# First block on whole float32 weights, weight splits moved to the second block, activation in two ScalarE steps, written-out order for the first block

## The chip, the cores and the metric

One core of a Trainium2 chip runs the whole program. The metric is device microseconds of one execution. TensorE multiplies, VectorE, ScalarE and GpSimd do elementwise work, and SyncE issues the DMAs. The kernel before took 884.1, 885.01 and 887.9 us in three runs, median 885.01.

## The reference

Attention without a softmax over the scores: `q` goes through a softmax over the head's 64 channels, `k` through one over the 576 positions, and out = q_s (k_sᵀ v). The result, 2304 tokens by 512, goes through two layers of the same shape:

```python
h = x @ w_in                       # 2304x512 @ 512x2048
g = where(h >= 1, h, where(h <= -1, 0, (h + 1)**2 / 4))
x = g @ w_out                      # 2304x2048 @ 2048x512
h = x @ w_in2
x = (h * tanh(log1p(exp(h)))) @ w_out2
```

The four weight matrices arrive as float64 and all else as float32. The kernel rebuilds each weight as float32 from its two 32-bit words.

## The kernel before, in words

The tokens are cut into six blocks of 384, the 2048 hidden channels into 16 chunks `c` of 128. The first layer runs in slots, one for each block `n` and chunk: `gemm1` (x times w_in, four slices of 128 channels into a bank `h`), the activation `act1`, `split_g`, and three slots later `gemm2` (w_out times g into four banks `acc`). While a block is worked on, the attention of later tokens is filled in between (tasks `kv_task` and `q_task`, one stage at a time). The second layer follows the sixth block; the change does not touch it.

A float32 product is made in one of two ways. `three` (L419) takes operands that were split into a high and a low part of the type float32r and issues three products. A plain float32 product is one line of code and two instructions in the trace. The kernel before uses the plain form in `gemm2` of the first block for the chunks under `WHOLE` = 8, and splits everywhere else.

A weight passes these stages (`w_stages`, 128x512 values at a time): DMA into `wraw`; VectorE `words` (L128, L132) builds a float32 magnitude from the two words; ScalarE rounds (L137), takes the sign (L138) and the magnitude (L143); `signed` multiplies the two (L155), on VectorE for most chunks and on GpSimd for the early ones; `w_parts` copies the high part on ScalarE (L202) and subtracts it on GpSimd (L204). A class `Line` moves the weights on by a stage per tick. In the first block all 32 weights of layer one pass through it; those of layer two follow, one every second slot.

The activation is three ScalarE steps from `h` (L459 to L461: half of the magnitude, half minus that and not under zero, square) and one on VectorE (L462). From chunk 8 on g is split too (L451, L452).

The order of the startup is a string, `STARTUP`, in which `p` with a number stands for that many products with the identity that fill TensorE's time. `REGIONS` says on which engines the order of issue is the order in the program: none up to slot 16, SyncE and ScalarE up to slot 80, all after that. Where it is not, a scheduler orders the instructions.

Of the kernel before, what the change touches and what calls it, by code (L numbers as in the profile page):

```python
# [18 lines left out]
P = 128  # L19
# [5 lines left out]
LEAD = 7  # L25
WHOLE = 8
REGIONS = [([], 0), ([], 16), (["sync", "scalar"], 16 * 5), (None, 16 * 6 + LAG)]
# [13 lines left out]
def tile_attention_two_moes(  # L41
# [77 lines left out]
    def w_stages(ph, c, m):  # L119
# [5 lines left out]
        def words():  # L125
# [10 lines left out]
            sg = f(t)[:, :, 1]  # L136
            nc.scalar.activation(out=sg, in_=sg, func=AF.Copy, bias=ROUND)  # L137
            nc.scalar.activation(out=sg, in_=sg, func=AF.Sign, bias=unround)  # L138

        def signed():  # L140
            t = f(st.pop("t"))
            w, sg = t[:, :, 0], t[:, :, 1]
            nc.scalar.activation(out=w, in_=w, func=AF.Abs)  # L143
            to = w
            if ph == 2:
                if c < NF // 2:
                    quarters[m, c] = big([P, 2, 2, 2 * P], F32, "wq")
                to = quarters[m, c % (NF // 2)][:, c * 2 // NF].rearrange("p c x -> p (c x)")
            elif m == 1 and c < WHOLE:
                if c % 2 == 0:  # L150
                    whole[c // 2] = big([P, 2, DM], F32, "whole")
                to = whole[c // 2][:, c % 2, :]
            st["w"] = to
# [3 lines left out]
        def split():  # L157
            if m == 0 or c >= WHOLE:
                w_parts(ph, c, m, st["w"])
# [33 lines left out]
        if ph == 1:  # L193
            return [words, signed, split]
        return [words, signed, sums, last_sum, store] if u >= 0 else [words, signed]
# [4 lines left out]
    def w_parts(ph, c, m, w, dve=False):  # L200
        t = parts[ph, c, m] = big([P, 2, DM], F32R, "parts")
        nc.scalar.activation(out=t[:, 0, :], in_=w, func=AF.Copy)  # L202
        eng = nc.vector if dve else nc.gpsimd
        eng.tensor_tensor(out=t[:, 1, :], in0=w, in1=f(t[:, 0, :]), op=ALU.subtract)  # L204
# [4 lines left out]
    def x_tiles(ph, n):  # L209
        xh[ph, n] = [small([P, 2, TB], F32R, "xh") for _ in range(NP // 2)]  # L210
# [10 lines left out]
    def by_rows(a, b, c, j0, nj, name):  # L221
# [17 lines left out]
    def kv_task(b, c):  # L239
# [4 lines left out]
        def load():  # L244
            st["k"], st["e"] = zip(*(by_rows(k, b, c + i, 0, J, "k_t") for i in two))
# [42 lines left out]

        def exps():
            st["e"] = [exp_tile(e, J, "k_e") for e in st["e"]]  # L290
            for i in two:
                kt = st["k"][i]
                mb = st["mb"][:R, i * P:(i + 1) * P].rearrange("p (h d) -> p h d", h=2)
                nc.vector.tensor_tensor(
                    out=kt, in0=kt, in1=mb.unsqueeze(2).to_broadcast([R, 2, J, D]), op=ALU.subtract
                )
                nc.scalar.activation(
                    out=st["e"][i].rearrange("p j h d -> p h j d"), in_=kt, func=AF.Exp
                )
# [26 lines left out]
        if not ready:  # L326
            return [load, load_v, rows_max, m_transpose, col_max, m_rows, exps, product, scaled]
# [5 lines left out]
    def q_task(b, c, nc_, j0, nj, n, o):  # L333
# [4 lines left out]
        def load():  # L338
            t = rows_tile("q_t")[:, :2 * nc_ * nj]
            if ready:  # L340
# [14 lines left out]
        def exps():  # L355
            g = st["g"]
            mx = sp.tile([R, 2 * J], F32, tag="qm", name="qm")[:, :2 * nc_ * nj]
            nc.vector.tensor_reduce(out=mx, in_=g, axis=AX.X, op=ALU.max)
            nc.gpsimd.tensor_tensor(
                out=g, in0=g, in1=mx.unsqueeze(2).to_broadcast([R, 2 * nc_ * nj, D]), op=ALU.subtract  # L360
            )
            if "e" in st:
# [9 lines left out]
        def scaled():  # L372
            g = st["e"].rearrange("p c j h d -> p (c j h) d")
            s = sp.tile([R, 2 * J], F32, tag="qs", name="qs")[:, :2 * nc_ * nj]
            nc.vector.tensor_reduce(out=s, in_=g, axis=AX.X, op=ALU.add)
            nc.vector.tensor_scalar_add(s, s, EPS)
            nc.vector.reciprocal(out=s, in_=s)
            nc.gpsimd.tensor_tensor(
                out=g, in0=g, in1=s.unsqueeze(2).to_broadcast([R, 2 * nc_ * nj, D]), op=ALU.mult
            )  # L380

# [21 lines left out]
        def x_split():  # L403
            ps = st["x"][:, :nc_ * w].rearrange("p (c t) -> p c t", c=nc_)
            if (1, n) not in xh:
                x_tiles(1, n)
            cs = slice(c % 2, c % 2 + nc_)
            hi, lo = xh[1, n][c // 2][:, cs, o:o + w], xl[1, n][c // 2][:, cs, o:o + w]
            nc.scalar.activation(out=hi, in_=ps, func=AF.Copy)
            nc.vector.tensor_tensor(out=lo, in0=ps, in1=f(hi), op=ALU.subtract)  # L410

        if not ready:
            return [load, exps, scaled, None, transposed, copied, product, x_split]
# [18 lines left out]
    def gemm1(s):  # L432
        ph, n, c = s
        hs[s] = h_p.tile([P, 512], F32, tag="h", name="h")
        for kc in range(NP):
            ks = slice(kc * P, (kc + 1) * P)
            three(
                hs[s][:, :TB], parts[ph, c, 0][:, 0, ks], parts[ph, c, 0][:, 1, ks],
# [571 lines left out]
```

## Time and profile before

| | |
|---|---|
| median of three runs | 885.01 us |
| the profiled execution | 884.33 us |
| its span | 882.5 us |
| TensorE busy | 847.6 us (96%) |
| VectorE, ScalarE, GpSimd busy | 570.2, 543.5, 412.6 us |

The span runs from the first to the last instruction that the profile shows; 1.83 us lie outside it. "Busy" of TensorE counts overlapping products until the modelled end of each, so a group's length is read from the start of one group to the start of the next.

### The profile page before, as it was taken

Reading aid. Unit: us, or ns where it says so; the run is one execution under the profiler, and the core shown is the slowest. Engines: PE = TensorE matmul, PEld = TensorE weight load, DVE = VectorE, ACT = ScalarE, POOL = GpSimd, SP = SyncE. Lnnn points to the kernel's source line nnn. Section 1 sums busy time; section 2 is a strip of 40 time slices with the busy share of each in tenths; the row PEclk is TensorE's granted clock in tenths of the full one; section 3 lists DMA queues with packets and bytes.
Section 4 is the critical chain, followed back from the end, with each engine's and each line's share of the span. In section 5 each row is a group of like instructions: output and inputs, shape, how many; then the busy total and the mean of one; then the engine's idle time right before and its main releaser. Section 6 shows DMA issues by size and latency. Waiting matters only on the chain. (4 is left out here: it accounts for less than half of the span.)

```text
span 882.5 us, 15027 instructions
## 1 busy us (share of the span) xinstructions
PE 847.6 (96%) x5308; PEld 820.9 (93%) x5308; DVE 570.2 (65%) x916; ACT 543.5 (62%) x953; POOL 412.6 (47%) x376
## 2 busy tenths in 40 slices
PE   7879779999999999999998999999999999999998
PEld 7756679899999999999998999999999999999998
DVE  6998975854756577475324636765667669656453
ACT  1899889877777777786756844442444466553521
POOL 2663666865645455364355316558555468000000
PEclk9799999999999999999999999999999999999999
DMA  9986221544664362354359238777876888866933
GB/s 251 325 235 166 72 58 51 170 134 131 163 186 135 105 206 94 117 170 141 110 206 341 61 102 272 253 269 286 306 247 248 317 316 293 279 225 197 305 113 103
DMA packets 139996, 171.27 MB, mean 194 GB/s; under 512 B 57360, under 2 KB 109584, under 8 KB 139920
## 3 DMA queue, kind: packets, MB, share of 16 engines
q1 hardware_dynamic: 139680, 170.10, 60.0%
q8 instruction: 42, 0.69, 0.3%
q14 instruction: 34, 0.28, 0.1%
q10 hardware_dynamic: 240, 0.20, 0.1%
HBM read 108.40 MB, written 61.87 MB: 193 GB/s over the span
## 5 line engine op out<-in xcount | busy, mean ns | idle before, releaser
L489 PE MATMUL acc<-ghl,parts 128*128 128x384 f32 x1056 | 204.0, 341 | 5.3 <-POOL v_t L250 2.6
L489 PEld LDWEIGHTS acc<-ghl,parts 128*128 128x128 f32 x1056 | 184.7, 189 | 7.6 <-POOL v_t L250 2.9
L690 PE MATMUL o<-w2p,gc 128*128 128x256 f32 x1296 | 152.8, 280 | 0.4 <-ACT gc L531 0.3
L690 PEld LDWEIGHTS o<-w2p,gc 128*128 128x128 f32 x1296 | 152.1, 189 | 0.8 <-ACT gc L531 0.8
L452 POOL TENSOR_TENSOR ghl<-rg,ghl 128x384 fp32r<-128x384 f32 x87 | 97.7, 1124 | 113.6 <-ACT ghl L451 110.5
L420 PE MATMUL h<-xh,parts 128*128 128x384 f32 x384 | 136.0, 354 | 7.6 <-DVE rg L462 7.6
L462 DVE SCALAR_TENSOR_TENSOR rg<-h,rg 128x384 f32<-128x384 f32 x96 | 53.2, 554 | 138.7 <-ACT rg L461 136.3
L422 PE MATMUL h<-xh,parts 128*128 128x384 f32 x384 | 132.2, 344 | 2.7 <-POOL parts L204 2.7
L421 PE MATMUL h<-xl,parts 128*128 128x384 f32 x384 | 131.5, 343 | 0.0
L531 ACT ACTIVATE gc<-gq 128x768 fp32r<-128x768 f32 x84 | 69.9, 843 | 64.0 <-DMA gq<-gd 43.5
L534 DVE TENSOR_TENSOR gc<-gq,gc 128x768 fp32r<-128x768 f32 x84 | 89.9, 1109 | 27.9 <-ACT gc L531 20.8
L421 PE MATMUL m<-xc,w2p 128*128 128x384 f32 x288 | 97.1, 337 | 1.3 <-DVE xc L534 1.3
L420 PE MATMUL m<-xc,w2p 128*128 128x384 f32 x288 | 97.1, 337 | 0.2 <-ACT xc L531 0.2
L422 PE MATMUL m<-xc,w2p 128*128 128x384 f32 x288 | 96.8, 336 | 0.0
L459 ACT ACTIVATE rg<-h 128x384 f32<-128x384 f32 x96 | 46.8, 487 | 63.1 <-PE h L422 61.1
L420 PEld LDWEIGHTS h<-xh,parts 128*128 128x128 f32 x384 | 73.7, 192 | 12.6 <-DVE rg L462 10.0
L627 ACT ACTIVATE high<-high 128x768 f32<-128x768 f32 x24 | 20.3, 847 | 94.2 <-DVE high L198 42.5
L422 PEld LDWEIGHTS h<-xh,parts 128*128 128x128 f32 x384 | 73.6, 192 | 4.7 <-POOL parts L204 4.5
L421 PEld LDWEIGHTS h<-xl,parts 128*128 128x128 f32 x384 | 73.7, 192 | 1.3
L132 DVE SCALAR_TENSOR_TENSOR wraw<-wraw 128x512 uint32<-128x512 uint32 x64 | 70.3, 1099 | 1.3
L198 POOL TENSOR_TENSOR s<-high 128x384 f32<-128x384 f32 x24 | 26.5, 1106 | 81.0 <-ACT high L627 81.0
L460 ACT ACTIVATE rg<-rg,half 128x384 f32<-128x384 f32 x96 | 59.4, 618 | 2.6
(110 smaller groups left out, 1562.3 us busy)
## 6 DMA issues: line engine op xcount, KB each, us to landing
gq<-gd SPq DMA_DIRECT2D x84, 384.0 KB, 6.1
gd<-s SPq DMA_DIRECT2D x48, 384.0 KB, 3.3
wraw<-in_moe_w_in_dram SPq DMA_DIRECT2D x32, 512.0 KB, 4.8
wraw<-in_moe_w_out_dram SPq DMA_DIRECT2D x32, 512.0 KB, 4.0
gd<-low SPq DMA_DIRECT2D x24, 384.0 KB, 3.8
wk<-ws SPq DMA_DIRECT2D x32, 256.0 KB, 2.1
w<-wk SPq DMA_DIRECT2D x16, 384.0 KB, 4.4
v_t<-in_v_dram SPq DMA_DIRECT2D x32, 144.0 KB, 3.4
```

The source lines that it names most:

```text
L132: nc.vector.scalar_tensor_tensor(out=t[:, :, 0], in0=t[:, :, 1], scalar=3, in1=t[:, :, 0], op0=ALU.logical_shift_left, op1=ALU.bitwise_xor,)
L420: nc.tensor.matmul(ps, ah, bh, start=start, stop=False)
L421: nc.tensor.matmul(ps, ah, bl, start=False, stop=False)
L422: nc.tensor.matmul(ps, al, bh, start=False, stop=stop)
L452: eltwise(s).tensor_tensor(out=gl[s], in0=g, in1=f(gh[s]), op=ALU.subtract)
L459: nc.scalar.activation(out=r, in_=h, func=AF.Abs, scale=0.5)
L460: nc.scalar.activation(out=r, in_=r, func=AF.Relu, scale=-1.0, bias=half)
L462: nc.vector.scalar_tensor_tensor(out=g, in0=h, scalar=0.0, in1=r, op0=ALU.max, op1=ALU.add)
L489: nc.tensor.matmul(acc[key][x][:, :TB], *pairs[at], start=first and at == 0, stop=last and at == 2)
L531: nc.scalar.activation(out=hi, in_=x, func=AF.Copy)
L534: eng.tensor_tensor(out=lo, in0=x, in1=f(hi), op=ALU.subtract)
L690: nc.tensor.matmul(ps[j][:, :QUARTER], a[:, c, js], b, start=i == c == which == 0 and b is wh, stop=i == pairs[-1] and c == which == 1,)
```

## The change

1. Layer one, first block (n = 0): x is not split, and `gemm1` and `gemm2` use the plain float32 form for all 16 chunks, on weights kept in `whole` tiles. The weights are not split in this block.
2. The weights of layer one are split in the second block: in slot c `w_high` copies and `w_low` subtracts for the w_in chunk c + 3 (subtraction on VectorE) and the w_out chunk c (on GpSimd). The first three w_in chunks are split at the end of the first block.
3. The activation is two ScalarE steps (a Relu with scale and bias, a square) and one on VectorE that takes max with 1 and min with the square. This holds in all blocks.
4. All multiplications of magnitude and sign of layer one are on GpSimd.
5. The weights of layer two start in the middle of the second block, two in three slots.
6. `STARTUP` now holds everything up to the end of the first block, with the attention of the second batch (names in capitals), and every engine keeps that order.

```diff
-REGIONS = [([], 0), ([], 16), (["sync", "scalar"], 16 * 5), (None, 16 * 6 + LAG)]
+AHEAD = 3
+REGIONS = [(["sync", "scalar"], 16 * 5), (None, 16 * 6 + LAG)]
 STARTUP = (
...
+    "w8.words w4.abs act0.c w4.mul w12.L w3.rnd act0.g w6.rnd w7.words w13.L Q0.L Q1.L G0 w3.sgn w6.sgn w10.words "
...
-            eng = nc.vector if (m if ph == 2 else c > (1 if m else 8)) else nc.gpsimd
-            eng.tensor_tensor(out=to, in0=w, in1=sg, op=ALU.mult)
+            eng = nc.vector if ph == 2 and m else nc.gpsimd
+            eng.tensor_tensor(out=to, in0=t[:, :, 0], in1=t[:, :, 1], op=ALU.mult)
...
+    def w_high(c, m):
...
+        t = parts[c, m] = big([P, 2, DM], F32R, "parts")
+        nc.scalar.activation(out=t[:, 0, :], in_=whole[m, c // 2][:, c % 2, :], func=AF.Copy)
+
+    def w_low(c, m):
+        t, w = parts[c, m], whole[m, c // 2][:, c % 2, :]
+        eng = nc.gpsimd if m else nc.vector
+        eng.tensor_tensor(out=t[:, 1, :], in0=w, in1=f(t[:, 0, :]), op=ALU.subtract)
...
+            if n == 0:
+                nc.tensor.matmul(
+                    hs[s][:, :TB], whole[0, c // 2][:, c % 2, ks], xh[ph, n][kc // 2][:, kc % 2, :],
+                    start=kc == 0, stop=kc == NP - 1,
+                )
+                continue
...
     def as_whole(s):
-        return s[:2] == (1, 0) and s[2] < WHOLE
+        return s[:2] == (1, 0)
...
-        nc.scalar.activation(out=r, in_=h, func=AF.Abs, scale=0.5)
-        nc.scalar.activation(out=r, in_=r, func=AF.Relu, scale=-1.0, bias=half)
-        nc.scalar.activation(out=r, in_=r, func=AF.Square)
-        nc.vector.scalar_tensor_tensor(out=g, in0=h, scalar=0.0, in1=r, op0=ALU.max, op1=ALU.add)
...
+        nc.scalar.activation(out=t[:, 0, :], in_=hs[s][:, :TB], func=AF.Relu, scale=0.5, bias=half)
...
+        nc.scalar.activation(out=r, in_=r, func=AF.Square)
...
+        nc.vector.scalar_tensor_tensor(
+            out=g, in0=hs[s][:, :TB], scalar=1.0, in1=r, op0=ALU.max, op1=ALU.min
+        )
...
-            elif ph == 1 and (n < NB - 1 or line.items):
-                w_tick(2 if c % 2 else 1)
...
+            if (n > 1 or n == 1 and c >= NF // 2) and (n < NB - 1 or line.items):
+                w_tick(i % 3)
...
+            if n == 1:
+                w = [(x, m) for x, m in ((c + AHEAD, 0), (c, 1)) if x < NF]
```

On TensorE the startup before runs as follows (`warm` is a product with the identity, `mT` and `mb` belong to the maxima of k, `kv` to the product of k and v, `qT` are transposes of q, `xps` is x before it is copied out):

```order
L841 MATMUL warm<-ident 128x128 x20
L268 MATMUL mT<-ident,km 128x96 x4
L841 MATMUL warm<-ident 128x128 x3
L284 MATMUL mb<-ident,mx 96x128 x2
L841 MATMUL warm<-ident 128x128
L284 MATMUL mb<-ident,mx 96x128 x2
L841 MATMUL warm<-ident 128x128 x34
L305 MATMUL kv<-v_t,k_e 128x130 x12
L386 MATMUL qT<-ident,q_e 128x96 x8
L305 MATMUL kv<-v_t,k_e 128x130 x12
L386 MATMUL qT<-ident,q_e 128x96 x8
L401 MATMUL xps<-qt,kvs_85 128x384 x2
```

and the changed kernel's startup runs so:

```order
L944 MATMUL warm<-ident 128x128 x33
L309 MATMUL mT<-ident,km 128x96 x2
L944 MATMUL warm<-ident 128x128 x12
L309 MATMUL mT<-ident,km 128x96 x2
L325 MATMUL mb<-ident,mx 96x128 x4
L944 MATMUL warm<-ident 128x128 x34
L351 MATMUL kv<-v_t,k_e 128x130 x24
L452 MATMUL qT<-ident,q_e 128x96 x8
L467 MATMUL xps<-qt,kvs_85 128x384
L452 MATMUL qT<-ident,q_e 128x96 x4
L467 MATMUL xps<-qt,kvs_86 128x384
L467 MATMUL xps<-qt,kvs_85 128x384
```

More identity products stand ahead of the first maxima, the two products of k and v stand together, and none of the transposes lies between them.

In the first block, TensorE's rows of the kernel before, around the first `gemm2` (L420 to L422 are `three`, L478 the plain form):

```order
L420 MATMUL h<-xh,parts 128x384
L421 MATMUL h<-xl,parts 128x384
L422 MATMUL h<-xh,parts 128x384
L478 MATMUL acc<-rg,whole 128x384 x4
L420 MATMUL h<-xh,parts 128x384
L421 MATMUL h<-xl,parts 128x384
L422 MATMUL h<-xh,parts 128x384
```

and the changed kernel's (L514 is `gemm1` on whole weights, L571 `gemm2`):

```order
L514 MATMUL h<-x_412,whole 128x384 x2
L514 MATMUL h<-x_413,whole 128x384 x2
L571 MATMUL acc<-rg,whole 128x384 x4
L514 MATMUL h<-x_412,whole 128x384 x2
L514 MATMUL h<-x_413,whole 128x384 x2
L571 MATMUL acc<-rg,whole 128x384 x4
L514 MATMUL h<-x_412,whole 128x384 x2
L514 MATMUL h<-x_413,whole 128x384 x2
L571 MATMUL acc<-rg,whole 128x384 x4
```

A slot of before has 12 products of split operands and four whole ones (12 split ones from chunk 8 on); a slot of the change has eight whole ones.

On ScalarE, a slot of the first block before (L202 is the copy of a weight's high part, L459 to L461 the activation):

```order
L137 ACTIVATE wraw<-wraw 128x512
L459 ACTIVATE rg<-h 128x384
L138 ACTIVATE wraw<-wraw,unround 128x512
L460 ACTIVATE rg<-rg,half 128x384
L143 ACTIVATE wraw<-wraw 128x512
L461 ACTIVATE rg<-rg 128x384
L202 ACTIVATE parts<-wraw 128x512
L137 ACTIVATE wraw<-wraw 128x512
L143 ACTIVATE wraw<-wraw 128x512
L138 ACTIVATE wraw<-wraw,unround 128x512
```

and the changed kernel's (L162, L166, L170 are round, sign and magnitude, L539 and L543 the activation):

```order
L162 ACTIVATE wraw<-wraw 128x512 x2
L166 ACTIVATE wraw<-wraw,unround 128x512 x2
L170 ACTIVATE wraw<-wraw 128x512
L539 ACTIVATE rg<-h,half 128x384
L170 ACTIVATE wraw<-wraw 128x512
L543 ACTIVATE rg<-rg 128x384
L162 ACTIVATE wraw<-wraw 128x512 x2
L166 ACTIVATE wraw<-wraw,unround 128x512 x2
```

The copy and one step of the activation have gone from the slot, and two weights pass in each.

## Rows read from the trace of the kernel before

**Rows 1.** Stages: busy of each engine (instructions), granted clock, DMA share, GB/s

```profile
core 0: us, PE busy (x) PEld busy (x) DVE busy (x) ACT busy (x) POOL busy (x), PEclk, DMA share, GB/s
22.00:34.00 12.00, 11.77 (x63) 11.50 (x64) 11.96 (x23) 9.16 (x16) 9.04 (x8) 0.57 0.98 312
38.00:158.00 120.00, 101.17 (x508) 86.77 (x507) 100.99 (x152) 111.41 (x209) 71.86 (x59) 0.96 0.47 132
158.00:600.00 442.00, 437.63 (x2530) 428.80 (x2529) 262.00 (x442) 295.19 (x545) 228.61 (x216) 1.00 0.53 170
```

**Rows 2.** TensorE's waits from 38 to 158 us: total, times, longest

```profile
PE h L420 <- DVE rg L462: 7.1, 4, 3.8
PE qT L386 <- DVE kvs L321: 3.4, 1, 3.4
...
PE acc L489 <- POOL v_t L250: 2.6, 1, 2.6
```

**Rows 3.** TensorE's timeline, first block and start of the second: start, duration

```profile
37.87 0.63 PE L421 MATMUL h<-xl,parts 128*128 128x384 f32 x1
...
55.66 2.74 PE L478 MATMUL acc<-rg,whole 128*128 128x384 f32 x8
58.20 0.41 PE L420 MATMUL h<-xh,parts 128*128 128x384 f32 x1
58.45 0.34 PE L421 MATMUL h<-xl,parts 128*128 128x384 f32 x1
...
152.66 0.34 PE L420 MATMUL h<-xh,parts 128*128 128x384 f32 x1
...
154.76 0.51 PE L489 MATMUL acc<-ghl,parts 128*128 128x384 f32 x2
...
157.61 0.34 PE L420 MATMUL h<-xh,parts 128*128 128x384 f32 x1
```

**Rows 4.** TensorE's timeline, startup

```profile
1.58 7.13 PE L841 MATMUL warm<-ident 128*128 128x128 f32 x40 [1.58 <-POOL ident masks.py:199]
...
12.76 7.76 PE L841 MATMUL warm<-ident 128*128 128x128 f32 x68
22.22 4.15 PE L305 MATMUL kv<-v_t,k_e 96*128 96x130 f32 x24 [1.71 <-issue]
```

**Rows 5.** TensorE's timeline, key-value products of the second batch

```profile
111.49 2.84 PE L305 MATMUL kv<-v_t,k_t 96*128 96x130 f32 x24
114.09 1.98 PE L489 MATMUL acc<-ghl,parts 128*128 128x384 f32 x10
```

**Rows 6.** ScalarE's groups by form, first 160 us: busy, mean

```profile
L460 ACT ACTIVATE rg<-rg,half 128x384 f32<-128x384 f32 x20 | 12.5, 623 | 0.2
```

**Rows 7.** ScalarE's timeline, one weight in the first block

```profile
46.18 0.70 ACT L143 ACTIVATE wraw<-wraw 128x512 f32<-128x512 f32 x1
46.74 0.78 ACT L138 ACTIVATE wraw<-wraw,unround 128x512 f32<-128x512 f32 x1
47.39 0.69 ACT L137 ACTIVATE wraw<-wraw 128x512 f32<-128x512 f32 x1
```

**Rows 8.** Instructions on raw weights, first 60 us: min/median/max ns

```profile
L128 DVE TENSOR_SCALAR wraw<-wraw x14: 413/430/4524, 18.0 to 59.1; 128x512 uint32<-128x512 uint32 x14
...
L132 DVE SCALAR_TENSOR_TENSOR wraw<-wraw x13: 678/694/2417, 18.4 to 56.3; 128x512 uint32<-128x512 uint32 x13
...
L155 POOL TENSOR_TENSOR wraw<-wraw x5: 1036/1221/1485, 28.5 to 54.3; 128x512 f32<-128x512 f32 x5
...
L204 POOL TENSOR_TENSOR parts<-wraw,parts x5: 1296/1304/1504, 31.3 to 57.3; 128x512 fp32r<-128x512 f32 x5
```

**Rows 9.** VectorE's groups by form, first 160 us: busy, mean

```profile
L132 DVE SCALAR_TENSOR_TENSOR wraw<-wraw 128x512 uint32<-128x512 uint32 x34 | 39.1, 1151 | 0.6
L128 DVE TENSOR_SCALAR wraw<-wraw 128x512 uint32<-128x512 uint32 x34 | 24.1, 712 | 3.7 <-DMA wraw<-in_moe_w_in_dram 2.1 <-DMA wraw<-in_moe_w_out_dram 1.6
...
L462 DVE SCALAR_TENSOR_TENSOR rg<-h,rg 128x384 f32<-128x384 f32 x19 | 10.5, 550 | 9.4 <-ACT rg L461 9.3
```

More of the change, by code (lines that the diff above doesn't have):

```diff
@@ L193, in w_stages, with first, second @@
         if ph == 1:
-            return [words, signed, split]
-        return [words, signed, sums, last_sum, store] if u >= 0 else [words, signed]
+            return dict(words=words, rnd=rounded, sgn=sign, abs=magnitude, mul=signed)
+        def first():
+            words()
+            rounded()
+            sign()
+        def second():
+            magnitude()
+            signed()
+        return [first, second, sums, last_sum, store] if u >= 0 else [first, second]
     def add(eng, out, a, b, sub=True):
         eng.tensor_tensor(out=out, in0=a, in1=b, op=ALU.subtract if sub else ALU.add)
[L200 to L203, printed above, removed]
+    def w_high(c, m):
[4 more added lines that the diff above has]
+        eng = nc.gpsimd if m else nc.vector
         eng.tensor_tensor(out=t[:, 1, :], in0=w, in1=f(t[:, 0, :]), op=ALU.subtract)
@@ L324, in scaled @@
                 )
-        if not ready:
-            return [load, load_v, rows_max, m_transpose, col_max, m_rows, exps, product, scaled]
+        if b < 2:
+            return dict(
+                L=load, V=load_v, max=rows_max, mT=m_transpose, mx=col_max, mb=m_rows, s0=partial(below, 0),
+                s1=partial(below, 1), e0=partial(exp, 0), e1=partial(exp, 1), kv=product, sc=scaled,
+            )
         return [
@@ L478, in gemm2 @@
                 nc.tensor.matmul(
-                    a[:, :TB], whole[c // 2][:, c % 2, x * P:(x + 1) * P], gh[s], start=first, stop=last
+                    a[:, :TB], whole[1, c // 2][:, c % 2, x * P:(x + 1) * P], gh[s], start=first, stop=last
                 )
@@ L801, in drain @@
                 self.step()
-    ahead = [(1, c, m) for c in range(NF) for m in range(2)]
-    ahead += [(2, c, m) for m in range(2) for u in range(NF // 2) for c in (u, u + NF // 2)]
+    ahead = [(2, c, m) for m in range(2) for u in range(NF // 2) for c in (u, u + NF // 2)]
     todo = list(ahead)
@@ L807, in tile_attention_two_moes, with w_ahead, w_tick @@
     fill = None
-    def w_ahead(upto):
-        while ahead and ahead[0][0] <= upto and len(raws) < (4 if upto == 1 else 1):
+    def w_ahead():
+        while ahead and len(raws) < 1:
             w_load(*ahead.pop(0))
-    def w_tick(upto):
-        line.tick(w_stages(*todo.pop(0)) if todo and todo[0][0] <= upto else None)
+    def w_tick(new):
+        line.tick(w_stages(*todo.pop(0)) if todo and new else None)
     def region(engines):
@@ L955, in tile_attention_two_moes @@
         put(places, end - 6 + 2 * i if i < 3 else end - 1, g_split, 0, i)
-    with region(REGIONS[0][0]):
+    with region(None):
         startup()
-    at = 0
-    for engines, upto in REGIONS[1:]:
+    at = NF
+    for engines, upto in REGIONS:
         with region(engines):
```

181 lines of the change are left out of this document (108 added, 73 removed), and 28 rows, old and new, of the table STARTUP.

## The prediction

> **What bounds the kernel now.** I read the busy time by stages first, then TensorE's waits, then its timeline where the change begins and ends, then the groups on ScalarE and VectorE there. From 158 to 600 us TensorE is busy 437.6 of 442 us: it sets the time, and a faster ScalarE or VectorE can win 4.4 us there at the very most [rows 1]. From 38 to 158 us it is busy 101 of 120, and even this counts overlapped ends; ScalarE is busy for 111 of the 120 us and VectorE for 101 [rows 1]. So the weights' conversion and splitting hold TensorE back there. Its longest waits are for VectorE's last step of the activation (7.1 us in four waits), for the scaled k-v products (3.4) and for a tile of v (2.6) [rows 2]. The rest is lost in the startup: between 22 and 34 us the granted clock is 0.57, mostly the lower of the levels 1.2 and 2.4 GHz, after TensorE had idled 1.7 us ahead of the first k-v product, whose 24 instructions then took 4.15 us [rows 1, 4]. The same 24 take 2.6 us at the full clock, from 111.49 to 114.09 [rows 5].
>
> The sum is made between two points that both kernels have: the start of the first `gemm1`, and the start of `gemm1` for the fifth chunk of the second block, which stands at 157.61 us [rows 3]. Behind that point TensorE has the same products to do in both kernels.
>
> **What a product costs.** A split `gemm1` or `gemm2` is 12 instructions and takes 2.10 us (152.66 to 154.76) [rows 3]. A whole one is eight instructions: they start at 55.66, and the second split product behind them starts at 58.45; less the 0.17 us of the one product between, they take 2.62 us [rows 3]. So a whole chunk costs 0.52 us more than a split one.
>
> Before, the stretch from 37.87 to 157.61 us holds 20 `gemm1` (16 of the first block, four of the second) and eight split `gemm2` of the first block with one of the second, 29 × 2.10 = 60.9 us; eight whole `gemm2`, 21.0 us; and the products of the second batch's attention. Of these the k-v products are two groups of 24, 2 × 2.6 = 5.2 us [rows 5]; the transposes, maxima and projections I estimate at as much again, so 10 us together. The sum is 92 of 119.7 us: some 28 us are waits and half clock.
>
> After, the same stretch holds 32 whole groups, 32 × 2.62 = 83.8 us, five split ones, 10.5, and the same 10: 104.3 us. The change thus adds 12.6 us of products (24 × 0.52), in exchange for waits.
>
> **What happens to ScalarE.** One weight takes it 0.56 + 0.65 + 0.56 us from start to start (magnitude, sign, and rounding like the magnitude) = 1.77 us [rows 7]. Two weights pass in a slot: 3.54 us. The Relu with a bias lasts 0.62 us and overlaps its neighbour by some 0.12, so 0.5, and the square no more [rows 6, 7]. That is 4.5 us in a slot whose products take 5.24. Before, the copy of the high part and the third step came on top, 0.6 to 0.9 and 0.4 us, against products of 4.7. ScalarE passes from bound to covered. VectorE has two weights at 0.43 + 0.69 us undisturbed [rows 8], at 0.71 + 1.15 as they were on average [rows 9], and 0.55 for the activation [rows 9]: 2.8 to 4.3 us. GpSimd has two multiplications of 1.04 to 1.49 us each [rows 8]. Both are under 5.24 with the attention's work on top, but VectorE not by much. If that cover goes, a slot grows by what is missing; the second rival prices it.
>
> **Startup.** The first group of 40 warm-up products ran from 1.58 to about 8.5 us, the later one of 68 in 7.8 us, 0.114 each [rows 4]. Now 66 come first, which puts the first maxima at 8.5 + 26 × 0.1 = 11 us; 24 more, the second maxima, and four products for the broadcast, about 4.5 us; then 68 more, 7.4 us: the k-v products can start at 23 us, about where they did (22.2). All 48 instructions follow on a TensorE that has not idled, so at 2.6 us for 24 they take 5.2 us instead of the 4.15 and 5.46 of before, until 28. VectorE's scaling, the transposes, copies and projections are a chain that took from 33.2 to 37.9 us before; with four copies in a row on ScalarE I take 6.3 us. The first `gemm1` starts at 34.5 us, 3.4 earlier than 37.87 [rows 3]. The bounds are 31 us (the chain as long as before, warm-ups a tenth faster) and 38 us (nothing won).
>
> **Waits that stay.** In the first slots VectorE has seven conversions between the scaling of k and v and the first activation, 7.8 to 13 us; the first two `gemm1` take 5.2, so the first `gemm2` comes 0 to 3.3 us late. The attention's waits can recur: they were 3.4 and 2.6 us [rows 2]. Together with the 7.1 us on the activation the upper bound is 13 us, the lower none. I take 6 us, near the two attention waits, since the activation now has a whole `gemm2` and `gemm1` between it and its use.
>
> **Second block.** All 32 splits of layer one lie here, two in a slot of 4.2 us of products: on ScalarE 2 × 0.6 us, with copy and activation of g 2.6 us, and 1.2 more from chunk 8 on for layer two's weights (two thirds of 1.77): 3.8. On GpSimd a subtraction for the weight (1.30 [rows 8]) and a like one for g, 2.5 us. They are wanted three slots later. I take nothing beyond the 6 us; without that cover each slot of the block's second half grows by about 1.2 us, 10 in all.
>
> **Later blocks.** One ScalarE step fewer is off the path; the earlier bound of 4.4 us is the most it can give, and I take none. SyncE issues the same DMAs earlier, mostly ahead of need: the stretch of before used 0.47 of the DMA engines [rows 1].
>
> **The sum.** 34.5 + 104.3 + 6 = 144.8 us for the point that stood at 157.61: 12.8 us won. The span goes from 882.5 to 869.7 and the execution, with 1.83 us outside it, from 884.33 to 871.5. The median of before lies 0.7 us above its profiled execution, less than my rounding.
>
> **A rule weighed.** The instructions on raw weights show that VectorE's shift takes 0.43 us by the median and 4.52 at worst, and its second step 0.69 and 2.42, while GpSimd works [rows 8]. Averaged, a weight's pair costs 1.86 instead of 1.12 us [rows 9]. The Trainium skill, SBUF — State Buffer, section "SBUF: two separate sides", says that VectorE (in some modes, or with two inputs from SBUF) and GpSimd lock one port pair for a whole instruction, and the loser waits. By that rule, the stretched rows agree, and putting all multiplications on GpSimd speaks against the change. The sum above would stand at VectorE's stretched rate, and fall at a full lock; that result is the second rival.
>
> **The rivals.**
> *No new waits.* The order is complete and all engines have slack, so the 6 us vanish: 871.5 − 6 = 865.5 us. For it: the slots' sums of 4.5 and 4.3 against 5.24. Against it: the seven conversions and the fill of the attention come in bursts.
> *VectorE and GpSimd take turns in the first block.* About 29 weights at 1.12 us and 30 multiplications at 1.04 [rows 8] are 63.7 us; the attention's row maxima and GpSimd's eight passes over q (some 13 us) and the first splits (5 us) make 82. Were none of VectorE's other work (16 × 0.55 [rows 9] and some 16 us of attention) hidden behind GpSimd, the block would take 107 us instead of 93.8. The point comes at 34.5 + 107 + 10.5 = 152, 5.6 us won: 878.7 us. For it: the 4.52 us row. Against: the average of 1.86 us leaves VectorE at 88 us of 94.
> *The turn-taking also binds the second block: slower.* There the port is wanted in a slot for a VectorE split (about 0.7 us) and two thirds of a weight (0.75), for GpSimd's 1.30, 1.1, 0.7 and nearly 1 us for q and the sums: 5.5 us against 4.2 from chunk 8 on. Eight slots lose 10 us on top of the second rival: 889 us. It decides from a loss of 12.8 us beyond my 6 in both blocks together. Against it: in the stretch from 158 us on, with a like mix but for the splits, TensorE lost 4.4 us in 442 [rows 1].
>
> **Chances.** The forecast (867 to 876) 0.60, no new waits 0.14, turns in the first block 0.18, turns in both 0.08. The likeliest case is 871.5 us. The range goes from 864, below the case without waits, to 881, which takes in the second rival and leaves out the third. About 0.5% (4.4 us) is what a measurement tells from no change: faster is all of the first two cases and most of the third, 0.88; same takes the rest of the third and part of the fourth, 0.07; slower 0.05.
>
> **What will show it.** In the changed profile `gemm1` of the first block takes 2.62 us in eight instructions and its first starts near 34.5 us; the granted clock stays at 1.0 from the k-v products on; the fifth `gemm1` of the second block starts near 145 us; ScalarE is no longer busy nine tenths of the first block; VectorE's shift averages 0.7 us or less. I am wrong if TensorE waits for GpSimd's multiplications or VectorE's activation in most slots, if an idle stretch brings the clock back to half during the block, or if TensorE loses more than a few us between 145 and 600 us.

## The result and the profile after

The changed kernel takes 872.41 us (median of 4 runs, 869.08 to 872.92) against 886.19 us (884.1 to 887.9) of the kernel before on the same chip: a ratio of 0.9838, 95% interval 0.9803 to 0.9873. The forecast was 871.5 us. The profiled execution took 872.6 us, with a span of 870.8; that of before, from which the forecast was summed, took 884.33.

First the stages, as in [rows 1]; one row is the stretch between the two points of the sum.

```profile
core 0: us, PE busy (x) PEld busy (x) DVE busy (x) ACT busy (x) POOL busy (x), PEclk, DMA share, GB/s
22.00:34.00 12.00, 11.75 (x95) 10.36 (x94) 10.54 (x28) 6.09 (x13) 5.16 (x5) 1.00 1.05 374
36.00:60.00 24.00, 23.26 (x73) 13.13 (x72) 21.67 (x31) 23.11 (x42) 12.94 (x11) 1.00 0.97 267
38.00:145.00 107.00, 103.95 (x410) 68.98 (x409) 79.72 (x130) 89.77 (x163) 55.46 (x52) 1.00 0.55 135
145.00:600.00 455.00, 448.55 (x2598) 441.42 (x2597) 282.72 (x466) 270.59 (x492) 248.29 (x231) 0.99 0.54 174
```

TensorE has gone from 84% busy (101.17 of 120) to 97% (103.95 of 107), ScalarE from 93% to 84%, and the granted clock of the startup from 0.57 to 1.00. Behind 145 us the clock is 0.99 where it was 1.00, and TensorE is idle for 6.5 of 455 us where it was for 4.4 of 442.

TensorE's waits from 36 to 145 us (total, times, longest) are all that is left of [rows 2]:

```profile
PE acc L571 <- DVE rg L548: 2.7, 2, 2.0
PE kv L351 <- PE h L514: 0.3, 1, 0.3
```

The wait for the k-v scaling (3.4 us) and that for v (2.6) are gone; one on the activation stays. TensorE's timeline (start, duration, then engine, line and tiles) holds the marks of [rows 3] and [rows 4]:

```profile
1.37 10.34 PE L944 MATMUL warm<-ident 128*128 128x128 f32 x66 [1.37 <-POOL ident masks.py:199]
11.55 0.33 PE L309 MATMUL mT<-ident,km 96*128 96x96 f32 x2
...
23.31 1.39 PE L351 MATMUL kv<-v_t,k_e 96*128 96x130 f32 x11
...
35.84 1.13 PE L514 MATMUL h<-x,whole 128*128 128x384 f32 x3
...
143.72 0.33 PE L496 MATMUL h<-xh,parts 128*128 128x384 f32 x1
...
505.18 0.34 PE L496 MATMUL m<-xc,w2p 128*128 128x384 f32 x1
```

The first `gemm1` stands at 35.84 us (37.87 before by [rows 3]), the fifth of the second block at 143.72 (157.61), and the first product of layer two at 505.18. The trace of before has its first `h` product at 35.52 and the first product of layer two at 520.27:

```profile
35.52 0.45 PE L420 MATMUL h<-xh,parts 128*128 128x384 f32 x1
36.80 1.53 PE L401 MATMUL xps<-qt,kvs 128*128 128x384 f32 x4 [0.83 <-DVE kvs L321]
...
520.27 0.34 PE L420 MATMUL m<-xc,w2p 128*128 128x384 f32 x1
```

The row at 37.87 is only the second product of its first `gemm1`: the first one stood alone at 35.52, ahead of projections that waited for the k-v scaling, and the other eleven ran from 37.87. Counted from that row, 2.0 us were won up to the first `gemm1`, 11.9 from there to the fifth of the second block, 1.2 from there to layer two (361.5 us instead of 362.7); layer two gave back 3.4 (365.6 instead of 362.2). The sum is 11.7, the difference of the spans (882.5 − 870.8).

On ScalarE and VectorE the groups by form of the first 160 us answer to [rows 6, 9] (last column but one: mean in ns):

```profile
L539 ACT ACTIVATE rg<-h,half 128x384 f32<-128x384 f32 x24 | 14.2, 594 | 20.5 <-PE h L498 12.1 <-PE h L514 8.4
...
```

```profile
L155 DVE SCALAR_TENSOR_TENSOR wraw<-wraw 128x512 uint32<-128x512 uint32 x32 | 29.0, 907 | 1.1
L151 DVE TENSOR_SCALAR wraw<-wraw 128x512 uint32<-128x512 uint32 x32 | 19.9, 623 | 0.1
```

ScalarE now stands idle 20.5 us ahead of the Relu, since TensorE has not yet made `h`: the wait has changed sides. VectorE's pair per weight takes 1.53 us on average, between the undisturbed 1.12 and the 1.86 of before.

Behind 145 us there is one new wait of size. The timelines of TensorE, ScalarE and VectorE around it:

```profile
187.06 0.50 PE L452 MATMUL qT<-ident,q_t 96*128 96x96 f32 x4
...
194.93 1.65 PE L467 MATMUL xps<-qt,kvs 128*128 128x384 f32 x2 [3.14 <-ACT qt L460]
...
196.69 0.52 PE L497 MATMUL h<-xl,parts 128*128 128x384 f32 x1
197.01 0.52 PE L498 MATMUL h<-xh,parts 128*128 128x384 f32 x1
```

```profile
190.09 0.68 ACT L162 ACTIVATE wraw<-wraw 128x512 f32<-128x512 f32 x1 [0.81 <-DVE wraw L155]
...
192.43 0.63 ACT L237 ACTIVATE parts<-whole 128x512 fp32r<-128x512 f32 x1 [0.86 <-POOL wq L183]
...
194.40 0.47 ACT L460 ACTIVATE qt<-qT 128x384 f32<-128x384 f32 x1
```

```profile
186.69 3.37 DVE L155 SCALAR_TENSOR_TENSOR wraw<-wraw 128x512 uint32<-128x512 uint32 x1
```

Read it from the end. TensorE's projection waits 3.14 us for ScalarE's copy of q, although the transpose that it copies was issued at 187.06. The copy starts at 194.40, 6.8 us after the transposes, because it stands in ScalarE's queue behind instructions for a weight of layer two and its neighbours. Two of these waited: 0.81 us for a VectorE instruction that lasted 3.37 us instead of 0.69, and 0.86 for a GpSimd multiplication. The other 5.2 us are ScalarE's own work ahead of the copy, so without the two waits TensorE would by these numbers still have stood for about 1.5 us. Then TensorE, which had idled 3.14 us, starts its products 0.32 us apart instead of 0.17, which is half speed, and the granted clock of 180 to 200 us is 0.91.

### The profile page after: what moved, and what is told of

It is laid out like the page before. It is cut to its first block, busy times and chain, and to the rows that moved or that the text cites. A ratio compares the mean times of both kernels' runs of the same rounds, so it can differ in the third digit from the quotient of the medians.

```text
span 870.8 us, 14851 instructions
## 1 busy us (share of the span) xinstructions
PE 853.1 (98%) x5276; PEld 807.0 (93%) x5276; DVE 563.0 (65%) x907; ACT 493.9 (57%) x849; POOL 400.5 (46%) x373
## 5 line engine op out<-in xcount | busy, mean ns | idle before, releaser
L582 PE MATMUL acc<-ghl,parts 128*128 128x384 f32 x960 | 183.0, 339 | 0.0
L582 PEld LDWEIGHTS acc<-ghl,parts 128*128 128x128 f32 x960 | 167.5, 188 | 1.1
L534 POOL TENSOR_TENSOR ghl<-rg,ghl 128x384 fp32r<-128x384 f32 x79 | 87.9, 1114 | 99.8 <-ACT ghl L533 85.7
L496 PE MATMUL h<-xh,parts 128*128 128x384 f32 x320 | 112.3, 351 | 0.5 <-DVE rg L548 0.5
L497 PE MATMUL h<-xl,parts 128*128 128x384 f32 x320 | 108.0, 337 | 0.1
L498 PE MATMUL h<-xh,parts 128*128 128x384 f32 x320 | 107.9, 337 | 0.0
L539 ACT ACTIVATE rg<-h,half 128x384 f32<-128x384 f32 x96 | 55.5, 578 | 70.7 <-PE h L498 62.2
L155 DVE SCALAR_TENSOR_TENSOR wraw<-wraw 128x512 uint32<-128x512 uint32 x64 | 64.1, 1002 | 1.9
L496 PEld LDWEIGHTS h<-xh,parts 128*128 128x128 f32 x320 | 60.5, 189 | 2.3 <-DVE rg L548 0.8
L497 PEld LDWEIGHTS h<-xl,parts 128*128 128x128 f32 x320 | 60.4, 189 | 1.9 <-DVE xl L479 0.4
L151 DVE TENSOR_SCALAR wraw<-wraw 128x512 uint32<-128x512 uint32 x64 | 40.7, 635 | 32.3 <-DMA wraw<-in_moe_w_out_dram 19.6
L498 PEld LDWEIGHTS h<-xh,parts 128*128 128x128 f32 x320 | 60.4, 189 | 0.0
```

What stands on the lines that cost most here:

```text
L151: nc.vector.tensor_scalar(out=t[:, :, 0], in0=t[:, :, 0], scalar1=29, scalar2=0x40000000, op0=ALU.logical_shift_right, op1=ALU.bitwise_xor,)
L155: nc.vector.scalar_tensor_tensor(out=t[:, :, 0], in0=t[:, :, 1], scalar=3, in1=t[:, :, 0], op0=ALU.logical_shift_left, op1=ALU.bitwise_xor,)
L496: nc.tensor.matmul(ps, ah, bh, start=start, stop=False)
L497: nc.tensor.matmul(ps, ah, bl, start=False, stop=False)
L498: nc.tensor.matmul(ps, al, bh, start=False, stop=stop)
L534: eltwise(s).tensor_tensor(out=gl[s], in0=g, in1=f(gh[s]), op=ALU.subtract)
```

## The experiments

All ratios are to the kernel before, run on the same chip in the same minutes. For the changed kernel that ratio is 0.9838. Marks from the trace are the first `gemm1` of the first block (35.84 in the changed kernel), the first of the second block (125.20), the fifth there (143.72) and the first product of layer two (505.18).

**Is the shorter activation what wins?** The three-step activation put back everywhere in the changed kernel:

```diff
-        nc.scalar.activation(out=t[:, 0, :], in_=hs[s][:, :TB], func=AF.Relu, scale=0.5, bias=half)
+        nc.scalar.activation(out=t[:, 0, :], in_=hs[s][:, :TB], func=AF.Abs, scale=0.5)
...
+        nc.scalar.activation(out=r, in_=r, func=AF.Relu, scale=-1.0, bias=half)
...
```

> The changed kernel with the activation of before (three ScalarE steps in all blocks). Theory (the first block is bound by TensorE's whole products, 5.24 us a slot, and ScalarE with 4.5 is covered): 4.9 us a slot are still covered, so 872 to 874 us. Rival (the shorter activation is what won): 878 us or more.

Measured 883.05 us (879.83 to 884.24), ratio 0.9968 [0.9951, 0.9986]. My theory fell: 10.6 us of the gain go with one ScalarE instruction of some 0.6 us per chunk. But only some 2.4 us of it lie in the first block (the fifth `gemm1` of the second at about 146); layer two begins at 515.6 instead of 505.2. To place the loss, the three steps were then put back behind the first block only (the same edit, under `s[:2] != (1, 0)`):

> The changed kernel with the three-step activation again in every block but the first; the first block keeps two steps. The run with three steps everywhere took 883.05 against 872.4. Theory: nearly all of that is lost behind the first block, where ScalarE's extra 0.62 us in each of 80 steps delays the copies and exponentials that TensorE waits for: 880 to 884, with the fifth gemm1 of the second block within 1.5 us of 143.7 and layer two's start 7 to 11 us later than 505.2. Rival: the loss is the first block's, and later waits were a result of its late end: 873 to 876.

Measured 882.97 us (878.04 to 884.86), ratio 0.9970 [0.9950, 0.9990]. Its fifth `gemm1` of the second block starts at 143.94, as in the changed kernel (143.72), and layer two at 512.8: 7.7 us later, 7.4 of them behind that `gemm1`. Both marks are as the theory had them. TensorE's waits from 150 to 505 us, first in the changed kernel, then with three steps later:

```profile
PE xps L467 <- ACT qt L460: 4.1, 3, 3.1
PE h L496 <- DVE rg L548: 0.5, 1, 0.5
```

```profile
PE xps L467 <- ACT qt L460: 5.3, 4, 2.7
PE h L496 <- DVE rg L553: 2.3, 5, 0.7
...
```

There are twelve waits instead of four, with 8.3 us instead of 4.6 when the three smaller ones are counted that are not shown; what is added are mostly waits of `gemm1` for the activation. That is 3.7 of the 7.4 us. The list counts a wait only from the modelled end of the product before. Both traces hold the same 2084 product instructions in this stretch; read from start to start, those that come over 0.12 us later than their usual spacing lose 16.2 us in 36 places with three steps and 10.7 in 26 without, 5.5 us more. The last 2 us are spread over smaller delays, and what causes them stays open.

The same edit alone, in the kernel before, with its old order:

```diff
-        nc.scalar.activation(out=r, in_=h, func=AF.Abs, scale=0.5)
-        nc.scalar.activation(out=r, in_=r, func=AF.Relu, scale=-1.0, bias=half)
+        nc.scalar.activation(out=r, in_=h, func=AF.Relu, scale=0.5, bias=half)
...
```

> The kernel before with the two-step activation alone. Theory (ScalarE holds the first block of before, 111 of 120 us busy; 0.4 us a slot less is 6 us): 880 to 884 us against 886. Rival (the shorter activation is what won): 876 us or less. Rival (VectorE binds there, not ScalarE): 885 to 887 us.

Measured 880.48 us (878.92 to 881.98), ratio 0.9947 [0.9930, 0.9963]. The time is in the theory's range, but not for its reason. The fifth `gemm1` of the second block and the first product of layer two stand at

```profile
160.33 0.34 PE L420 MATMUL h<-xh,parts 128*128 128x384 f32 x1
...
518.23 0.34 PE L420 MATMUL m<-xc,w2p 128*128 128x384 f32 x1
```

against 157.61 and 520.27 in the kernel before. The first block, which was to gain 6 us, did not get shorter, though ScalarE's busy time from 38 to 158 us fell from 111.4 to 102.2 us. The gain lies behind it: from the one mark to the other it takes 357.9 us instead of 362.7. In this kernel a scheduler orders the first block and can order it anew after the edit, so the run does not show by itself what held that block.

**Do the unsplit weights win without the written order?** All sixteen second weights unsplit in the kernel before, in its old order:

```diff
-WHOLE = 8
+WHOLE = 16
```

> The kernel before with one part of the change alone: all sixteen second weights of the first block multiplied unsplit instead of eight, in the old order, the first weights still split from the start. Takes about 8 ScalarE copies (0.68 us each) and 8 subtractions out of the first block and puts them into the second, and makes 8 gemm groups of 2.1 us into 2.62 us on TensorE (4.2 us more). Theory: the first block before was held by ScalarE and by waits (116 us of products in 136 us), so the products fit into the idle time and the copies saved show: 882 to 885. Rival: the waits come from the order in which the work stands and stay, the products are added: 887 to 891.

Measured 883.16 us (880.61 to 885.11), ratio 0.9973 [0.9955, 0.9992]: within the theory's range. TensorE's waits from 30 to 150 us show why no more comes of it:

```profile
PE h L420 <- DVE rg L462: 7.9, 5, 3.8
PE xps L401 <- DVE kvs L321: 3.0, 1, 3.0
```

Those of [rows 2] on the activation and the k-v scaling are still there. Its marks are 155.0 and 517.7 us, both 2.6 earlier than before, so here the gain is in the first block. In the opposite experiment the changed kernel's startup and first block are left to the scheduler:

```diff
-    with region(None):
+    with region([]):
         startup()
```

> The changed kernel with the startup and first block ordered by the scheduler instead of by the written order. Theory (the arithmetic wins, the order only trims waits): 871 to 877 us. Rival (the written order is what won): 880 us or more.

Measured 892.66 us (891.0 to 893.01), ratio 1.0081: slower than before, as the rival had it. The loss is in front of the first block:

```profile
PE mb L325 <- DVE mx L317: 5.4, 2, 4.5
PE qT L452 <- POOL q_e L440: 3.7, 1, 3.7
...
```

```profile
52.09 1.54 PE L514 MATMUL h<-x,whole 128*128 128x384 f32 x2
```

These are its waits from 10 to 55 us and its first `gemm1`: 52.09, 16.3 us later than in the changed kernel. The waits listed for that stretch make 10.9 us, and the granted clock from 10 to 52 us is 0.82. From there to the fifth `gemm1` of the second block it needs some 112 us instead of 107.9 (119.7 before), so the order saves only some 4 us in the block itself, and most of the block's gain comes without it.

**Do VectorE and GpSimd hold each other up?** 21 of the weights' multiplications go back from GpSimd to VectorE:

```diff
-            eng = nc.vector if ph == 2 and m else nc.gpsimd
+            eng = nc.vector if (m if ph == 2 else c > (1 if m else 8)) else nc.gpsimd
```

> The changed kernel with 21 of the 32 multiplications of magnitude and sign of layer one back on VectorE, as before. Theory (moving them off VectorE is needed for the cover; VectorE is busy 80 of 107 us in the first block): some 20 us more there, so waits come back, 875 to 880 us. Rival (VectorE has room, or is relieved of turns with GpSimd): 871 to 873 us.

Measured 870.80 us (870.27 to 873.52), ratio 0.9844: no difference, next to the rival's forecast. VectorE's groups of the first 160 us show how it took on 15.1 us of work:

```profile
L155 DVE SCALAR_TENSOR_TENSOR wraw<-wraw 128x512 uint32<-128x512 uint32 x32 | 26.4, 824 | 1.1
L151 DVE TENSOR_SCALAR wraw<-wraw 128x512 uint32<-128x512 uint32 x32 | 16.0, 499 | 0.0
L183 DVE TENSOR_TENSOR whole<-wraw 128x512 f32<-128x512 f32 x21 | 15.1, 726 | 4.6 <-ACT wraw L170 4.5
```

The two steps on the raw weights became 6.5 us shorter (42.4 instead of 48.9) when GpSimd did 21 multiplications fewer beside them, which fits VectorE having waited for it in that time. A multiplication costs 1.18 us on GpSimd and 0.73 on VectorE.

**Which engine is the first block's next bound?** Two kernels leave work out. In the first, two of the four slices of each `gemm1` of the first block are left out, which takes some 21 us of products away:

```diff
+            if n == 0 and kc % 2:
+                continue
...
```

> The changed kernel with two of the four slices left out of each gemm1 of the first block. A slot then has 3.9 us of products, 1.3 us less. Theory (TensorE sets the slots, ScalarE with 4.5 us right behind it): ScalarE takes over, the first block shortens by some 10 of the 21 us, about 862 us. Rival (the slots were not TensorE's): 869 us or more. Rival (ScalarE is far from binding): 852 us.

Measured 865.23 us (865.07 to 865.39). The second block begins at 122.1 instead of 125.2, and the first `gemm1` at 34.7 instead of 35.8: of the 21 us the first block itself gives back 1.9. In its stages VectorE is as good as always busy until 100 us, and TensorE waits for its activation step (8.3 us in four waits):

```profile
36.00:60.00 24.00, 18.86 (x52) 10.29 (x52) 21.70 (x31) 22.61 (x41) 13.13 (x12) 0.93 0.98 277
60.00:80.00 20.00, 14.79 (x45) 8.26 (x44) 19.52 (x31) 14.86 (x27) 8.52 (x10) 0.91 1.08 233
80.00:100.00 20.00, 17.84 (x99) 13.07 (x98) 19.40 (x37) 18.43 (x32) 10.71 (x11) 1.00 0.56 122
```

The forecast of a bound by ScalarE was wrong on the time (by 3 us) and on the engine. The second kernel also leaves out VectorE's second step on the raw weights of layer one:

```diff
-            nc.vector.scalar_tensor_tensor(
+            if ph == 2: nc.vector.scalar_tensor_tensor(
```

> Leaves out, beside two of the four slices of every gemm1 of the first block, the second of the two integer operations with which VectorE makes a weight word of layer one (L155). In the run with half of gemm1 VectorE was busy 60.6 of the 64 us to 100 us, and this operation took 24.6 us of it (26 of 948 ns). Theory: VectorE is the second bound of the first block, right behind TensorE; without the operation the block ends when ScalarE (77.3 of 86 us busy there) lets it, so the first gemm1 of the second block comes at 113 to 117 us instead of 122.1 and the time is 857 to 861. Rival: the written order or the arrival of the weights holds the block, and VectorE's busy time was only waiting: the mark stays at 120 to 122 and the time at 863.5 to 866.

Measured 857.22 us (856.46 to 857.98), and the second block begins at 114.3: another 7.8 us, as the theory had it. The granted clock, 0.93 and 0.91 in the first two stages above, is 1.00 here, so a part of the 7.8 us may be the clock's. Its stages:

```profile
36.00:60.00 24.00, 20.33 (x61) 10.89 (x60) 10.48 (x21) 24.00 (x44) 13.05 (x13) 1.00 0.92 258
60.00:80.00 20.00, 16.28 (x58) 9.19 (x57) 15.96 (x29) 19.40 (x35) 9.17 (x12) 1.00 1.03 234
80.00:100.00 20.00, 19.42 (x107) 14.33 (x106) 12.93 (x33) 19.62 (x37) 13.10 (x13) 1.00 0.75 151
```

Now ScalarE is the busy one (63.0 of 64 us). So, read together, TensorE, VectorE and ScalarE stand close behind one another in this block.

**What do the first warm-ups cost?** 66 warm-up instructions (33 products) stand ahead of the first maxima. The changed kernel's VectorE had those ready and waited:

```profile
8.78 0.29 DVE L304 TENSOR_TENSOR km<-km,km 96x128 f32<-96x128 f32 x1
11.92 0.36 DVE L317 TENSOR_REDUCE mx<-mT 128x2 f32<-128x192 f32 x1 [2.85 <-PE mT L309]
```

The number in `pN` counts products, each two instructions; 16 products fewer, and four more where the v tiles arrive later:

```diff
-k1.max p33 k0.mT
+k1.max p17 k0.mT
-w0.words p34 k0.kv
+w0.words p38 k0.kv
```

> The changed kernel with 17 instead of 33 warm-up products ahead of the first maxima of k and 38 instead of 34 behind them. Theory (VectorE stood 2.9 us until the warm-ups let the first maxima through): the first gemm1 starts 2 to 3 us earlier and the time is 869 to 870.5 us. Rival (the k-v products wait for v or for the exponentials, and a gap brings the half clock): 872 us or more.

Measured 869.01 us (868.3 to 869.63), ratio 0.9822 [0.9806, 0.9838]: the time as expected, and the fastest kernel that computes everything, though its interval overlaps that of the changed kernel. Its marks:

```profile
7.97 0.33 PE L309 MATMUL mT<-ident,km 96*128 96x96 f32 x2
...
34.40 0.81 PE L514 MATMUL h<-x,whole 128*128 128x384 f32 x2
```

The maxima come 3.6 us earlier, and 1.4 us of that reach the first `gemm1`, where 2 to 3 were expected. The kernels with the longer warm-up in the written order have their first `gemm1` at 34.7 to 36.0 us, and the two with the shorter one at 34.4 and 34.1, so the 1.4 us are no more than the longer one's own spread, though both shorter ones lie below all of it. The profiled execution lies 4.3 us under that of the changed kernel: 0.9 at the start of layer two (504.3), 3.4 behind it. So the edit itself has shown 0.9 to 1.4 us in the traces; the rest is layer two's varying part, told below. With the 21 multiplications on VectorE as well:

> The shorter warm-up of the earlier run (869.0) with 21 of the weights' multiplications back on VectorE (870.8 alone, against 872.4 of the changed kernel). Theory: the two engines trade the same time back and forth in the first block, so the second edit gives nothing: 868 to 870, and the sum of its VectorE busy time in the first block is again larger by 6 to 8 us without more waits of TensorE. Rival: the 1.6 us that the second edit seemed to give are real and add up: 866 to 868.

Measured 871.51 us (869.17 to 873.56), ratio 0.9845 [0.9815, 0.9874]. Neither forecast's range holds the median; the theory's is nearer, and the two gains do not add. Its first `gemm1` is at 34.1, yet layer two starts at 505.2: the earlier start is lost again.

**Can the new wait at 194.93 be taken away?** One more half slot between the copy of q and the projection:

```diff
...
-transposed, copied, product, None,
-            x_split,
+transposed, copied, None, product,
+            None, x_split,
```

> The changed kernel with one more half slot between the copy of transposed q and its projection in the attention tasks of blocks three to six. Theory (what the later blocks lose is TensorE standing at the projection while ScalarE is behind, 3.1 us once at 195 us and the half clock behind it): about 2 of the 3.1 us and the half clock go, 868 to 870 us. Rival (ScalarE is behind as a whole and the wait moves to the next product): 871 to 873 us.

Measured 872.97 us (871.48 to 875.21), ratio 0.9867: by the time, the rival. From 145 to 505 us the waits for the copy fall from 4.1 to 1.2 us, and those of `gemm1` for the low part of x rise from none to 3.0:

```profile
PE h L497 <- DVE xl L479: 3.0, 3, 2.2
PE xps L467 <- ACT qt L460: 1.2, 2, 0.8
```

In the one trace the stretch from the fifth `gemm1` to layer two is 1.1 us shorter than in the changed kernel (360.3 instead of 361.5), and the first block, which the edit does not touch, 1.4 us longer. So a gain of about a microsecond is neither shown nor ruled out.

Then the conversion of layer two's weights, which stands ahead of that copy, was begun in the third block instead of the middle of the second:

```diff
-if (n > 1 or n == 1 and c >= NF // 2) and (n < NB - 1 or line.items):
+if n > 1 and (n < NB - 1 or line.items):
-w_tick(i % 3)
+w_tick(i % 4)
```

> The changed kernel with the weights of layer two starting in the third block, three in four slots, so that the splits have the second block's ScalarE and VectorE alone. Theory (splits and layer two's weights together put ScalarE behind in the second block): the wait at 195 us goes, 867 to 870 us, unless three in four slots bring waits of their own. Rival (the wait comes from the attention's order alone): 871 us or more.

Measured 880.88 us (880.23 to 883.72), ratio 0.9962: the time was wrong, and the theory's proviso came true. The wait of 3.1 us is gone (TensorE busy 80.00 of 80 us from 145 to 225), but the work now fills three of every four slots in the later blocks. In the three stages from 225 to 440 us TensorE is busy 72.72 of 75, 66.43 of 70 and 66.53 of 70 us, and layer two begins at 512.4, 7.2 us later.

## Why the prediction was right, and where it was not

**The sum held.** The point at 144.8 us came at 143.72, the time of 871.5 at 872.41. That it came so near is partly luck: against the sum the startup was off by +1.3 us, the products by +0.4, the waits by −2.8, the later blocks by −1.2 and layer two by +3.4, together the 1.1 us by which the profiled execution lies above the forecast. The steps:

- *Products.* 104.3 us were summed. The stretch took 107.9 us, of which some 3.2 are waits, so about 104.7 are products. A whole group takes 2.58 us where nothing waits (43.66 to 46.24) against the 2.62 put down. Of the prediction's own arithmetic, 24 × 0.52 is 12.5, not 12.6.
- *Waits.* 6 us were taken and some 3.2 came. The two attention waits after which I sized them did not recur; what recurred is VectorE's activation step (1.96 and 0.74 us, at 70.46 and 52.31). The first `gemm2`, which was to come up to 3.3 us late, did not wait. So the 6 us were of about the right size for a wrong reason.
- *Startup.* 34.5 us forecast, 35.84 measured. The 37.87 to which the prediction compared it is the second product of that `gemm1`, as said above; the sum does not rest on it. The k-v products were forecast at 23 us and came at 23.31, and took 5.53 us instead of 5.2. The chain behind them took 7.0 us instead of the 6.3 that I had put down. The clock held at 1.00, as the step said. That I took the 66 warm-ups as given, where they hold back the first maxima, left out a term: moving them was worth about 1.4 us there.
- *Layer two* was taken as unchanged; the profiled execution lost 3.4 us in it. At 571.81 us TensorE waits for ScalarE and then for VectorE:

```profile
571.81 0.44 PE L496 MATMUL m<-xc,w2p 128*128 128x384 f32 x1 [1.03 <-ACT xc L624]
572.81 0.44 PE L497 MATMUL m<-xc,w2p 128*128 128x384 f32 x1 [0.56 <-DVE xc L627]
...
573.86 0.53 PE L496 MATMUL m<-xc,w2p 128*128 128x384 f32 x1
```

The products behind are at 0.53 us, and from 560 to 580 us the granted clock is 0.91. It need not come from the change: of the kernels with the written order, the trace of the shorter warm-up and that of it with the multiplications take 362.2 us for layer two, as before; the two with three steps take 365.2 and 365.9. In six of the fourteen traces, one of them of the old order, the granted clock from 560 to 600 us is 0.96, and layer two takes 364.4 to 366.0 us; in the other eight it is 1.00, and layer two takes 361.1 to 364.7. The four runs of the changed kernel split likewise: 869.08 us with a mean clock of 1.0, and 872.2 to 872.9 with 0.994 to 0.996. What decides it in an execution is open.

**The step that was mis-sized: "one ScalarE step fewer is off the path" in the later blocks.** I bounded it by the 4.4 us in which TensorE idles there in the kernel before, and took none. From the fifth `gemm1` of the second block to layer two, one trace each takes:

| | three steps | two steps |
|---|---|---|
| splits and order of before | 362.7 us | 357.9 us |
| splits and order of the change | 368.9 us | 361.5 us |

So the step is worth 4.8 us in the kernel before, about as much as the bound, and 7.4 in the changed kernel. Kernels that are the same in this stretch differ by up to 2.2 us (361.5 to 363.7 in four), so both gains are clear of the "none" that I took. Down the columns, the work that the change moves behind the first block costs 6.2 us with three steps and 3.6 with two. I had left out both, the cost and the gain, and they cancel: measured, the stretch won 1.2 us. That the moved splits and conversions are what makes the step worth more fits these numbers, but the change also differs in order.

**The second block** was taken at nothing beyond the 6 us. It did not lose the 10 us of the case without cover; what came is the one wait of 3.14 us near its end and the products at half clock behind it. The sign of being wrong that "TensorE loses more than a few us between 145 and 600 us" was thereby nearly met, with 6.5 us idle.

**What the parts are worth together.** Alone in the kernel before, two steps give a ratio of 0.9947 and eight more unsplit weights 0.9973. The changed kernel without the two steps has 0.9968, without the written order 1.0081, and whole 0.9838. The parts do not add: 0.5% and 0.3% stand against 1.6%. Of the 11.9 us won from the first `gemm1` to the fifth of the second block, 4.2 go when the scheduler orders it and 2.7 with three steps. What is left, some 5 us, would be the whole-weight `gemm1` and the splits moved out, but no run has these two alone: that share is a remainder and not shown. Caution is due on one more point: the written order was made for two steps, so the run with three shows the loss with an order that does not fit them. And that ScalarE's load bounds the first block of before, from which the prediction started, is not borne out by the two steps alone, which took 9.2 us of busy time off ScalarE there and left the block no shorter.

**The rivals.** *No new waits*: it was half true (3.2 of 6 us went). *Turns in the first block* did not decide, since TensorE's 104 us stand just above VectorE's load; but the cover was thinner than "leaves VectorE at 88 us of 94" tells. VectorE is busy 21.67 of the 24 us from 36 on, 19.52 and 19.40 of 20 after that and 10.82 of the last 25, and with half of `gemm1` gone the block shrank by 1.9 us only. *Turns in both blocks* has its mark in one place, the 3.37 us of L155 at 186.69; it held ScalarE for 0.81 us of the queue behind which TensorE waited 3.14.

**The rule on the shared port.** In that place VectorE's step of 0.69 us begins while a GpSimd instruction runs, and ends after two more of GpSimd's:

```profile
186.33 1.22 POOL L406 TENSOR_TENSOR q_t<-q_t,qm 96x512 f32<-96x512 f32 x1
187.51 0.74 POOL L232 TENSOR_TENSOR ws<-wq,ws 128x256 f32<-128x256 f32 x1
188.21 1.30 POOL L242 TENSOR_TENSOR parts<-whole,parts 128x512 fp32r<-128x512 f32 x1
189.47 1.47 POOL L534 TENSOR_TENSOR ghl<-rg,ghl 128x384 fp32r<-128x384 f32 x1
```

From 189.47 to its end at 190.06 are 0.59 us, nearly its own duration, and the GpSimd instruction that begins there is longer than its mean of 1.11 us. This agrees with the Trainium skill, SBUF — State Buffer, section "SBUF: two separate sides": a VectorE instruction with two inputs from SBUF and a GpSimd instruction that reads SBUF take one port pair for a whole instruction, and the other waits. That VectorE's steps became 6.5 us shorter when 21 multiplications left GpSimd points the same way; no run here separates the port from other causes.

**The order** had no term of its own in the sum. Measured against the scheduler's, it is worth 16.3 us ahead of the first block and some 4 us in it: without it the change would have made the kernel slower.

## What to carry to other kernels

The idle time of the engine that bounds, read in the kernel before, is a poor bound on what an instruction "off the path" is worth after a change: the same ScalarE step was worth 4.8 us before and 7.4 where other work had moved into its queue. A time in the forecast range does not show the mechanism: two steps alone came out at 880.48 us as expected, with the gain in another stretch than expected, and only marks in the trace tell. Where three engines stand within some per cent of each other, taking work from one gives little (here 1.9 of 21 us) until the next is relieved too, so parts are tried together as well as alone. Look for what a long queue delays: a copy of 0.47 us that stood in order behind other work and 1.7 us of waits came 6.8 us after its input and cost TensorE 3.14 us, and half clock after it.

## What had not been expected

- The two-step activation alone shortens the later blocks of the kernel before by 4.8 us and its first block not at all, though ScalarE had looked like the bound of that block.
- Warm-up products can be too many: 34 instead of 66 instructions ahead of the first maxima left the clock of the startup at 1.00 and brought the first `gemm1` forward by 1.4 us.
- Layer two takes 361 to 366 us in executions of kernels that are the same from there on. Of two kernels whose marks at 505 us agree, one can so be 3.4 us faster in a single execution; the shorter warm-up's lead of 3.4 us over the changed kernel is in good part of this kind.
